# Gate and up products written to PSUM in the order of the weights, with the stride moved into VectorE's transposes

## The chip, the cores and the metric

One core of a Trainium2 chip. The metric is the device time of one execution in microseconds (us), taken as the median of several executions. The kernel is one decode step of a transformer block: 84.2 MB are read from HBM and 1.25 KB are written.

## The reference, cut to what matters

```python
x = A_x                                          # [1, 1, 640], bf16
h = x + attention(layernorm(x), k_cache, v_cache, wq, wo)   # 32 heads of 128, 4096 cached positions
n = layernorm(h)
g = n @ w_gate                                   # 640 -> 1728
u = n @ w_up                                     # 640 -> 1728
h2 = h + (gelu(g) * u) @ w_down                  # 1728 -> 640
```

Everything below is about the last three lines, some 10 us at the end of a kernel of about 205 us.

## The kernel before

1728 = 13 * 128 + 64. In this kernel VectorE and ScalarE take gate and up as columns (128x15 in the timeline below): 128 partitions, with 13 numbers in each (plus two half-used columns for the remaining 64). TensorE makes rows: with the normed vector as the stationary operand (128*1 in the timeline), one matmul gives a row of outputs (416 of them here) along one partition of PSUM. Four such matmuls, at partitions 0, 32, 64 and 96, run side by side: in the trace of before the four start 3 to 4 ns apart, and the next four follow 0.305 us after the first of them. VectorE's transposes (0.68 us for 480 columns) are used here in blocks of 32x32: in the kernel's layout 32 neighbouring columns of a row become 32 partitions.

Partition p of the result is to hold the outputs 13p to 13p+12, since w_down is loaded so that each partition reads 13 whole rows in one piece. A row holds the outputs in the order of the weights: position 13n + c, for n in 0..31. For that layout a block has to take all n of one c side by side. Something has to take a stride of 13, and in this kernel it is the matmul's output:

```python
    def up(ps, w, name):          # 40 matmuls: 5 chunks of the 640 inputs x (four of 416, four of 64 columns)
        landed_once(name)                               # wait for the weights' load
        for j in range(DC):
            for last in range(2):
                for r in range(YR):
                    row = ps[32 * r : 32 * r + 1, :]
                    if last:                            # the remaining 64 outputs, repeated to fill 64 columns
                        ...
                    else:                               # RG = 13 * 32 = 416
                        rhs = w[:, j, r * RG : (r + 1) * RG].rearrange("p (n c) -> p n c", c=FULL)
                        to = row[:, 0:RG].rearrange("q (c n) -> q n c", c=FULL)   # neighbours 32 floats apart
                    inst = PE.matmul(to, lhsT=hc[:, j : j + 1], rhs=rhs, start=False, ...)

    PE.wait_ge(S["dve"], D_HC)
    end("g", up(g_ps, wg_sb, "wg"))
    fill(5)                                             # matmuls that only keep TensorE busy
    end("u", up(u_ps, wu_sb, "wu"))
    fill(4)
    PE.wait_ge(S["dve"], D_HID)
    down = {FULL: "wd0", 0: "wd1", WD[1][0]: "wd2", WD[2][0]: "wd3"}   # WD = ((0, 8), (8, 11), (11, 13))
    for c in range(NFC):                                # 14 groups of four matmuls in all
        if c in down:
            landed_once(down[c])                        # w_down comes in four loads
        ...
```

VectorE's side, with `ps` of 480 columns (416 and 64):

```python
    def turn_rows(col, ps):
        dve(lambda: DVE.transpose(col[:].rearrange("p c n -> p (c n)"), ps), False)
    ...
    wait_pe(T["end", "g"])
    turn_rows(g_col, g_ps)
    ...                     # 1/sd from GpSimd, gelu in nine small operations, with one exp on ScalarE between them
    wait_pe(T["end", "u"])
    turn_rows(u_col, u_ps)
    dve(lambda: DVE.tensor_tensor(hid[:], g_sb[:], u_col[:, :, 0], op=ALU.mult))     # the hidden vector
    wait_pe(T["end", "y"])
    DVE.tensor_tensor(y_row[:], y_ps, h_row[:], op=ALU.add).then_inc(S["y"], 1)      # then the store
```

And the end of the queue of loads, all issued by about 168 us:

```python
    load("wg", wg_sb, ...)
    load("wu", wu_sb, ...)
    SP.wait_ge(S["pe"], ...)                            # the K tile is free
    for i, (a, b) in enumerate(WD):                     # 1280, 480 and 320 KB
        load(f"wd{i + 1}", wd_sb[:, a:b, :], wd_rows[:, a:b, :])
    load("wd0", wd_last, ...)                           # 80 KB
```

The softmax here doesn't subtract the row's maximum and nothing guards it: scores larger than these inputs give would overflow.

Of the kernel before, what the change touches and what calls it, by code (L numbers as in the profile page):

```python
# [9 lines left out]
def kernel(  # L10
# [19 lines left out]
    PE, DVE, ACT, SP, POOL = nc.tensor, nc.vector, nc.scalar, nc.sync, nc.gpsimd  # L30
# [22 lines left out]
    FULL = DF // P  # L53
    LAST = DF - FULL * P
    PER = 2
    NFC = FULL + PER
    HALVES = D // PER
    COLS = NFC * HP
    WD = ((0, 8), (8, 11), (11, 13))
    RG = FULL * HP  # L60
# [102 lines left out]
    def tick(which, inst):  # L163
        inst.then_inc(S[which], 1)
        done[which] += 1
        return done[which]
# [6 lines left out]
    def wait(engine, which, value):  # L173
        if value > 0:
            engine.wait_ge(S[which], value)
# [8 lines left out]
    def landed_once(name):  # L184

        PE.wait_ge(S[name], 16)
        once.append(name)

    def wait_pe(value):
        DVE.wait_ge(S["pe"], value)  # L190

    def dve(make, raw=True):

        if raw:
            wait(DVE, "dve", done["dve"])
        return tick("dve", make())
# [132 lines left out]
    n = EV_RS  # L329
# [15 lines left out]
    n = 0  # L345
# [81 lines left out]
    D_RS = D0 + 4  # L427
    D_SPREAD, D_ROW, D_H, D_HC = D_RS + 4, D_RS + 5, D_RS + 8, D_RS + 10
    D_HV = D_HC + 3
    D_T1 = D_HV + 5  # L430
    D_HID = D_T1 + 7

    def fill(n):

        for _ in range(n):
            PE.matmul(  # L436
                s_bank[0][:], lhsT=ident[:], rhs=e_t[:].rearrange("p j i -> p (j i)"), start=True, stop=True
            )
# [27 lines left out]
    def up(ps, w, name):  # L466


        landed_once(name)
# [4 lines that stand above are left out]
                    if last:  # L474
                        first = FULL * P + r * (HP // PER)
                        rhs = w[:, j, first : first + HP // PER]
                        rhs = rhs.unsqueeze(1).unsqueeze(3).broadcast_to([P, PER, HP // PER, PER])
                        to = row[:, RG:COLS].rearrange("q (b i n) -> q b i n", b=PER, n=PER)
                    else:
                        rhs = w[:, j, r * RG : (r + 1) * RG].rearrange("p (n c) -> p n c", c=FULL)  # L480
                        to = row[:, 0:RG].rearrange("q (c n) -> q n c", c=FULL)
                    inst = PE.matmul(  # L482
                        to,
                        lhsT=hc[:, j : j + 1],
                        rhs=rhs,
                        start=False,
                        stop=(j == DC - 1),
                        skip_group_check=True,
                        tile_position=(0, 32 * r),
                    )  # L490
        return inst

    PE.wait_ge(S["dve"], D_HC)
    end("g", up(g_ps, wg_sb, "wg"))
    fill(5)
# [3 lines that stand above are left out]
    down = {FULL: "wd0", 0: "wd1", WD[1][0]: "wd2", WD[2][0]: "wd3"}  # L499
    order = range(NFC)  # L500
    for c in order:
        if c in down:
            landed_once(down[c])
        for r in range(YR):
            if c < FULL:
                w = wd_sb[:, c, r * YW : (r + 1) * YW]
            elif r // 2 == c - FULL:
                w = wd_last[:, (r % 2) * YW : (r % 2 + 1) * YW]
# [94 lines left out]
    for m in range(NQ):  # L603
        for g in ON_ACT:
            act_copy(m, g)
        for half in range(2):
            ACT.wait_ge(S["pe"], pe_at(m, ("s", half)))
            cols = slice(half * NB // 2, (half + 1) * NB // 2)
            for i in range(QH):
                r, h = slice(i * HP, (i + 1) * HP), QH * m + i  # L610
# [3 lines left out]
            inst.then_inc(S["act_pe"], 1)  # L614
    ACT.wait_ge(S["dve"], D_T1)
    ACT.activation(e2[:], t1[:], AF.Exp, scale=TWO_SQRT_2_OVER_PI).then_inc(S["act"], 1)
# [65 lines left out]
        dve_copies(m + 1, {})  # L682

    def turn_rows(col, ps):
        dve(lambda: DVE.transpose(col[:].rearrange("p c n -> p (c n)"), ps), False)  # L685

    assert done["dve"] == D0
    wait_pe(pe_at(NQ - 1, ("s", 1)))
# [18 lines left out]
    assert var_of(hm, hv) == D_HV  # L707
    wait_pe(T["end", "g"])
    turn_rows(g_col, g_ps)
    DVE.wait_ge(S["r"], 2)  # L710
    dve(lambda: DVE.tensor_scalar(g_sb[:], g_col[:, :, 0], hr[:], None, op0=ALU.mult))
    dve(lambda: DVE.tensor_tensor(t1[:], g_sb[:], g_sb[:], op=ALU.mult))
    dve(lambda: DVE.tensor_scalar(t1[:], t1[:], GELU_C, 1.0, op0=ALU.mult, op1=ALU.add))
    assert dve(lambda: DVE.tensor_tensor(t1[:], t1[:], g_sb[:], op=ALU.mult)) == D_T1
    DVE.wait_ge(S["act"], ACT_ALL)
# [4 lines left out]
    dve(lambda: DVE.scalar_tensor_tensor(g_sb[:], g_sb[:], hr[:], units[:], op0=ALU.mult, op1=ALU.mult))  # L720
    wait_pe(T["end", "u"])
    turn_rows(u_col, u_ps)
    assert dve(lambda: DVE.tensor_tensor(hid[:], g_sb[:], u_col[:, :, 0], op=ALU.mult)) == D_HID
    wait_pe(T["end", "y"])
# [46 lines left out]
```

## Time and profile before

| | before |
|---|---|
| time, median of 3 runs | 205.59 us (205.56 to 205.65) |
| span of the profiled run | 203.8 us |
| gate's 40 matmuls, up's 40 | 2.06 us each |
| one transpose of 480 columns | 0.68 us |
| end of `hc` (input of gate and up) to end of `hid` | 6.26 us |
| last landing of w_down | 200.51 us |
| start of the last group of down-projection matmuls | 200.55 us |

The page of the kernel before: the span, and three of its rows over 40 equal slices of 5.1 us. PEclk is the granted TensorE clock in tenths, DMA the busy share of the DMA engines in tenths, GB/s what they moved.

```profile
span 203.8 us, 7457 instructions
...
PEclk9999999955599559955995599559955995896699
DMA  7999999999999999999999999999999999999991
GB/s 249 394 476 418 390 485 408 412 453 428 434 426 402 436 428 425 444 431 431 431 418 421 448 431 437 431 431 431 431 437 431 405 428 447 444 394 437 428 384 49
```

The DMA engines are at 90% or more in 38 of the 40 slices. The kernel streams from HBM from start to end, so the first question about any change at its tail is when the last load lands.

Two views answer it. First the loads of w_down in the DMA view, with size and the time from issue to landing (the two last ones):

```profile
big<-in_B_w_down_dram SPq DMA_DIRECT2D x1, 320.0 KB, 32.9
big<-in_B_w_down_dram SPq DMA_DIRECT2D x1, 80.0 KB, 32.6
```

Then the queue's timeline: when the last of them was issued (start and duration in us).

```profile
167.89 0.44 SPq L548 DMA_DIRECT2D big<-in_B_w_down_dram  x1
```

167.89 + 32.6 is about 200.5; the trace's own record of landings has 200.51. The piece before it (columns 11 and 12) landed at 200.30.

The timeline of the tail before: start, duration, engine, line, operation, what it writes and reads, shape, count, and in brackets the idle time of the engine before it and what ended it.

```profile
193.00 0.23 DVE L706 TENSOR_SCALAR hc<-h_col,hm 128x5 bf16<-128x5 f32 x1
...
193.29 2.06 PE L482 MATMUL tp_103<-big,hc 128*1 128x416 bf16 x40
...
195.41 0.68 DVE L685 STREAM_TRANSPOSE g_col<-tp_103 128x480 f32<-128x480 f32 x1 [1.60 <-PE tp_103 L482]
196.20 0.23 DVE L711 TENSOR_SCALAR g_sb<-g_col,hr 128x15 f32<-128x15 f32 x1
...
196.47 2.06 PE L482 MATMUL tp_104<-big,hc 128*1 128x416 bf16 x40
...
198.25 0.23 DVE L720 SCALAR_TENSOR_TENSOR g_sb<-g_sb,hr,units 128x15 f32<-128x15 f32 x1
...
198.59 0.68 DVE L685 STREAM_TRANSPOSE u_col<-tp_104 128x480 f32<-128x480 f32 x1
199.31 0.18 DVE L723 TENSOR_TENSOR hid<-g_sb,u_col 128x15 bf16<-128x15 f32 x1
...
199.55 1.24 PE L455 MATMUL tp_105<-big,hid 128*1 128x160 bf16 x56
200.84 0.32 DVE L725 TENSOR_TENSOR y_row<-tp_105,h_row 128x160 bf16<-128x160 f32 x1 [1.35 <-PE tp_105 L455]
```

The starts of the single matmuls in the trace add what this merged view hides. In the down-projection (L455) a group of four follows every 69 ns, from first matmul to first matmul, except for the group of column 11, which comes after 106 ns, at 200.34, and the last one, which comes after 140 ns, at 200.55: each 40 ns behind the landing of its weights. (The prediction below has 96 and 130 ns. These are counted from the last matmul of the group before, where an ordinary gap is 59 ns, so they should not be set beside 69.) So the tail already waits for w_down, by about 0.1 us, though the bracket that would say so is absent. The ends of matmuls are modelled in the profile: it lets the matmul before the last group end at 200.65, after the landing at 200.51, so TensorE does not count as idle there. For the same reason the page's chain of work that ended last does not name the load either:

```profile
PE 18%; ACT 4%; DVE 1%; issue 0%
ACT ex L611 4%; PE tp_103 L255 3%; PE tp_104 L255 2%; PE tp_106 L255 2%; PE tp_105 L255 2%; PE o L281 2%; PE sa L436 2%; PE sa L268 2%; PE tp_103 L482 1%; PE tp_104 L482 1%; PE a L292 1%; PE tp_105 L455 1%; DVE u_col L685 0%; PE tp_106 L304
```

### The profile page before, as it was taken

Reading aid. Unit: us, or ns where it says so; the run is one execution under the profiler, and the core shown is the slowest. Engines: PE = TensorE matmul, PEld = TensorE weight load, DVE = VectorE, ACT = ScalarE, POOL = GpSimd, SP = SyncE. Lnnn points to the kernel's source line nnn. Section 1 sums busy time; section 2 is a strip of 40 time slices with the busy share of each in tenths; the row PEclk is TensorE's granted clock in tenths of the full one; section 3 lists DMA queues with packets and bytes.
Section 4 is the critical chain, followed back from the end, with each engine's and each line's share of the span. In section 5 each row is a group of like instructions: output and inputs, shape, how many; then the busy total and the mean of one; then the engine's idle time right before and its main releaser. Section 6 shows DMA issues by size and latency. Waiting matters only on the chain. (4 is left out here: it accounts for less than half of the span.)

```text
span 203.8 us, 7457 instructions
## 1 busy us (share of the span) xinstructions
PE 152.3 (75%) x3453; PEld 139.1 (68%) x3453; DVE 70.6 (35%) x163; ACT 81.6 (40%) x179; POOL 20.3 (10%) x20
## 2 busy tenths in 40 slices
PE   0003689854996399869985998389849989998994
PEld 0001179754996399869975998389849989997332
DVE  4003127300480049104800670038105801742452
ACT  0000326531386118623770477018712862674000
POOL 8301000620000000800000008000000000000010
PEclk9999999955599559955995599559955995896699
DMA  7999999999999999999999999999999999999991
GB/s 249 394 476 418 390 485 408 412 453 428 434 426 402 436 428 425 444 431 431 431 418 421 448 431 437 431 431 431 431 437 431 405 428 447 444 394 437 428 384 49
DMA packets 4058, 84.38 MB, mean 414 GB/s; under 512 B 464, under 2 KB 592, under 8 KB 848
## 3 DMA queue, kind: packets, MB, share of 16 engines
q1 hardware_dynamic: 4048, 84.23, 96.8%
q8 instruction: 8, 0.13, 0.3%
q14 instruction: 2, 0.02, 0.0%
HBM read 84.23 MB, written 0.00 MB: 413 GB/s over the span
## 5 line engine op out<-in xcount | busy, mean ns | idle before, releaser
L281 PE MATMUL o<-ex,big 128*128 128x4 bf16 x1024 | 29.7, 166 | 11.5 <-ACT ex L611 6.5
L281 PEld LDWEIGHTS o<-ex,big 128*128 128x128 bf16 x1024 | 28.3, 102 | 12.9 <-ACT ex L611 7.7
L597 ACT COPY big<-tp_104 128x1024 bf16<-128x1024 bf16 x16 | 16.2, 1012 | 48.3 <-PE tp_104 L255 48.3
L255 PE MATMUL tp_103<-ident,big 128*128 128x128 bf16 x256 | 24.9, 255 | 10.9 <-PEq L180 10.9
L255 PEld LDWEIGHTS tp_103<-ident,big 128*128 128x128 bf16 x256 | 20.4, 118 | 11.4 <-issue 11.4
L255 PE MATMUL tp_104<-ident,big 128*128 128x128 bf16 x256 | 24.1, 249 | 0.0
L255 PE MATMUL tp_105<-ident,big 128*128 128x128 bf16 x256 | 23.3, 244 | 0.0
L255 PE MATMUL tp_106<-ident,big 128*128 128x128 bf16 x256 | 23.1, 242 | 0.0
L624 DVE COPY big<-tp_103 128x1024 bf16<-128x1024 bf16 x24 | 16.5, 688 | 18.5 <-PE tp_103 L255 18.5
L542 POOL COPY wo<-wo_in 128x5120 bf16<-128x5120 bf16 x3 | 13.3, 4450 | 94.2 <-PE a L292 94.2
L255 PEld LDWEIGHTS tp_104<-ident,big 128*128 128x128 bf16 x256 | 19.9, 115 | 0.0
L255 PEld LDWEIGHTS tp_105<-ident,big 128*128 128x128 bf16 x256 | 19.2, 112 | 0.0
L255 PEld LDWEIGHTS tp_106<-ident,big 128*128 128x128 bf16 x256 | 18.9, 111 | 0.0
L268 PE MATMUL sb<-q_78,big 128*128 128x4 bf16 x512 | 14.3, 164 | 5.0 <-issue 5.0
L624 DVE COPY big<-tp_106 128x1024 bf16<-128x1024 bf16 x24 | 16.6, 691 | 3.4 <-PE tp_106 L255 2.9
L597 ACT COPY big<-tp_105 128x1024 bf16<-128x1024 bf16 x16 | 16.2, 1014 | 3.0 <-PE tp_105 L255 2.9
L268 PEld LDWEIGHTS sb<-q_78,big 128*128 128x128 bf16 x512 | 13.6, 96 | 5.1 <-issue 5.1
L611 ACT ACTIVATE ex<-sa 32x64 bf16<-32x64 f32 x32 | 9.8, 306 | 11.4 <-PE sa L268 11.2
L268 PE MATMUL sa<-q_78,big 128*128 128x4 bf16 x512 | 14.0, 164 | 0.0
L624 DVE COPY big<-tp_105 128x1024 bf16<-128x1024 bf16 x16 | 11.1, 691 | 8.4 <-PE tp_105 L255 8.1
L268 PEld LDWEIGHTS sa<-q_78,big 128*128 128x128 bf16 x512 | 13.5, 96 | 0.6
L681 DVE COPY o_raw<-o 128x4 f32<-128x4 f32 x4 | 0.7, 163 | 36.9 <-PE o L281 36.9
(111 smaller groups left out, 117.3 us busy)
## 6 DMA issues: line engine op xcount, KB each, us to landing
big<-in_A_v_cache_dram SPq DMA_DIRECT2D x8, 4096.0 KB, 33.1
big<-in_A_k_cache_dram SPq DMA_DIRECT2D x7, 4096.0 KB, 26.1
big<-in_A_wq_dram SPq DMA_DIRECT2D x1, 5120.0 KB, 15.5
wo_in<-in_A_wo_dram SPq DMA_DIRECT2D x4, 1280.0 KB, 27.1
big<-in_A_k_cache_dram SPq DMA_DIRECT2D x2, 2048.0 KB, 23.9
big<-in_B_w_gate_dram SPq DMA_DIRECT2D x1, 2160.0 KB, 39.0
big<-in_B_w_up_dram SPq DMA_DIRECT2D x1, 2160.0 KB, 43.6
big<-in_B_w_down_dram SPq DMA_DIRECT2D x1, 1280.0 KB, 31.8
```

The source lines that it names most:

```text
L255: inst = PE.transpose(tp_b[g % NBANK][:, b * DH : (b + 1) * DH], kt[slot][:, g * GRP + b, :], ident[:])
L268: inst = PE.matmul(s_ps[half][:, j % (NB // 2), :], lhsT=kt[slot][:, j, :], rhs=q8[:, slot * QH : (slot + 1) * QH], start=True, stop=True,)
L281: inst = PE.matmul(o_ps, lhsT=vt[slot][:, j, :], rhs=e_t[:, j, :], start=(j == 0), stop=(j == NB - 1))
L542: POOL.tensor_copy(wo_t[:], wo_in[:]).then_inc(S["wo"], 1)
L597: ACT.copy(group(m % SLOTS, g), tp_g[g % NBANK]).then_inc(S["act_pe"], 1)
L611: inst = ACT.activation(e_t[r, cols, i], s_ps[half][r, :, i], AF.Exp, scale=SCALE, accum_out=rs_all[r, half, h : h + 1])
L624: DVE.tensor_copy(group(m % SLOTS, g), tp_g[g % NBANK]).then_inc(S["dve_pe"], 1)
L681: event(DVE.tensor_copy(o_raw[:, HG * turn : HG * turn + QH], o_ps))
```

## The change

Its intent: TensorE writes its 416 columns at unit step, and VectorE, whose transpose of `h_col` already reads at a step of 20 bytes (0.47 us), takes the step of 13 floats (52 bytes). The 64 remaining columns were in another order already, so each transpose becomes two.

```diff
-    D_T1 = D_HV + 5
-    D_HID = D_T1 + 7
+    D_T1 = D_HV + 6
+    D_HID = D_T1 + 8
@@ in up()
-                        rhs = w[:, j, r * RG : (r + 1) * RG].rearrange("p (n c) -> p n c", c=FULL)
-                        to = row[:, 0:RG].rearrange("q (c n) -> q n c", c=FULL)
+                        rhs = w[:, j, r * RG : (r + 1) * RG]
+                        to = row[:, 0:RG]
@@ in turn_rows()
-        dve(lambda: DVE.transpose(col[:].rearrange("p c n -> p (c n)"), ps), False)
+        dve(lambda: DVE.transpose(col[:, 0:FULL], ps[:, 0:RG].rearrange("q (p c) -> q c p", c=FULL)), False)
+        dve(lambda: DVE.transpose(col[:, FULL:NFC].rearrange("p c n -> p (c n)"), ps[:, RG:COLS]), False)
```

Nothing else moves; the number of matmuls stays, and VectorE has two instructions more.

## The prediction

> **What bounds the kernel now.** The slices show the DMA engines at 90% or more up to the last slices (84.2 MB in a span of 203.8 us). The chain of waits names short PE, ScalarE and VectorE pieces at the end, but what counts is a load: in the DMA view the last piece of w_down is issued at 167.9 us and lands 32.6 us later, at about 200.51. The down-projection's matmuls agree: groups of four follow each other every 69 ns from 199.55, but the one that needs the third w_down piece comes after 96 ns (landing 200.30) and the last after 130 ns, at 200.55, 40 ns after the last landing. So it already waits about 0.1 us for weights. An earlier hidden vector gains nothing; one later by up to 0.1 us costs nothing.
>
> **PE: removed.** In the timeline a step of gate (four 416-column matmuls, four 64-column ones) takes 0.378 us: 0.305 from the 416s to the 64s, 0.07 for those, at a granted clock of 1.00. 0.305/416 is 0.73 ns a column; the 160-column matmuls with unit-stride output take 0.069/160 = 0.43. [...] With unit stride the 416s should take about 0.18: 0.13 us less a step, 0.65 for each of gate and up. Gate's saving moves the first transpose from 195.41 to about 194.76 (POOL's rstd ends before, at 194.44). Up's saving is worth nothing: up then ends near 197.2, long before VectorE asks.
>
> **VectorE: added.** One transpose of 480 unit-stride columns takes 0.683 us, so about 0.18 fixed. The strided transpose that exists (h_col, 160 columns, 20-byte step, SBUF) takes 0.469, where unit rate would give 0.35: 0.71 cycles more per element, as between the two reductions of the same 128 elements, 0.27 and 0.37. I assume the same for the 52-byte step in PSUM: 416 columns take 0.93 us (0.62 if the stride is free there, 1.1 if it costs double). The 64-column transpose takes 0.25, of which 0.08 may overlap. Together 1.10 us (0.8 to 1.3), against 0.68.
>
> **Critical path.** The gate chain from the transpose's end to the gated product, 2.39 us, stays. Up's transpose now runs right behind it. Down-projection starts at 194.76 + 1.10 + 2.39 + 0.04 + 1.10 + 0.28 = about 199.67, against 199.55. The exchange nearly cancels: +0.84 on VectorE, -0.65 on gate's matmuls, -0.1 of slack at up. The last group of four would start at 200.57, against 200.55 set by the loads. At 0.8 for the pair the time is unchanged, at 1.3 it is +0.4.
>
> **Predicted time:** 205.7 us, 205.4 to 206.2. Faster by over 2%: 0.005; within 2%: 0.985; slower by over 2%: 0.01.
>
> **What would show it.** Right: gate's and up's matmul groups fall from 2.06 to about 1.4 us; the strided transpose is 0.93 us; no VectorE idle before up's transpose; down-projection starts within 0.3 us of 199.55; last landing still 200.5. Wrong on the loads: an earlier down-projection ends earlier. Wrong on VectorE: a strided transpose of 0.62 (time unchanged, longer waits for w_down) or over 1.1.
>
> **What would make it wrong.** PE now idles about 1.6 us before down-projection; if the clock falls, its groups take 121 to 133 ns, as in the attention projection at 0.50, and the end moves by 0.8.

0.18 us is 416 times the 0.43 ns a column read off the 160-column groups. That the stride is what makes the 416s slow was inference from 0.73 against 0.43 ns; the run of after bears it out. The 0.18 us fixed and the unit rate of VectorE's transposes were estimates too, shown only later: in after_probes 64, 160 and 416 columns at unit step in SBUF took 245, 346 and 611 ns, which makes 1.04 ns per element and 0.18 us fixed. A cycle in its VectorE paragraph stands for that 1.04 ns.

## The result, and the profile after

| | before | after |
|---|---|---|
| time, median of 6 runs each | 205.62 us (205.48 to 206.26) | 205.55 us (205.43 to 205.69) |
| ratio, 95% interval | | 0.999 (0.9976 to 1.0004) |
| gate's matmuls, up's matmuls | 2.06, 2.06 us | 1.20, 1.20 us |
| transposes of gate, from the first start to the last end | 0.68 us | 0.75 us |
| end of `hc` to end of `hid` | 6.26 us | 5.33 us |
| last landing of w_down | 200.51 us | 200.38 us |
| last group of down-projection starts | 200.55 us | 200.42 us |

A ratio here is the mean time of one kernel's fast runs over that of the other's in the same rounds, so it is not quite the ratio of the medians quoted.

The time is the same. The chain of small steps that the change touches is 0.93 us shorter, and none of it arrives. The page after:

```profile
span 203.7 us, 7459 instructions
...
PEclk9999969955695569856985698569855995995797
DMA  7999999999999999999999999999999999999991
GB/s 249 418 452 418 394 482 409 415 454 451 415 410 412 455 409 431 438 438 438 418 418 427 442 431 438 438 438 418 425 444 431 409 425 447 438 400 437 427 386 50
```

The stream of loads looks as it did. The timeline of the tail after:

```profile
192.41 0.23 DVE L708 TENSOR_SCALAR hc<-h_col,hm 128x5 bf16<-128x5 f32 x1
...
192.69 1.20 PE L482 MATMUL tp_103<-big,hc 128*1 128x416 bf16 x40
...
193.94 0.62 DVE L686 STREAM_TRANSPOSE g_col<-tp_103 128x416 f32<-128x416 f32 x1 [0.73 <-PE tp_103 L482]
194.48 0.21 DVE L687 STREAM_TRANSPOSE g_col<-tp_103 128x64 f32<-128x64 f32 x1
194.80 0.23 DVE L713 TENSOR_SCALAR g_sb<-g_col,hr 128x15 f32<-128x15 f32 x1
...
195.16 1.20 PE L482 MATMUL tp_104<-big,hc 128*1 128x416 bf16 x40
...
196.85 0.23 DVE L722 SCALAR_TENSOR_TENSOR g_sb<-g_sb,hr,units 128x15 f32<-128x15 f32 x1
197.00 0.61 DVE L686 STREAM_TRANSPOSE u_col<-tp_104 128x416 f32<-128x416 f32 x1
197.53 0.21 DVE L687 STREAM_TRANSPOSE u_col<-tp_104 128x64 f32<-128x64 f32 x1
197.78 0.19 DVE L725 TENSOR_TENSOR hid<-g_sb,u_col 128x15 bf16<-128x15 f32 x1
...
198.35 0.72 PE L455 MATMUL tp_105<-big,hid 128*1 128x160 bf16 x32 [1.02 <-DMA big<-in_B_w_down_dram]
...
199.42 0.38 PE L455 MATMUL tp_105<-big,hid 128*1 128x160 bf16 x12 [0.35 <-DMA big<-in_B_w_down_dram]
...
200.22 0.45 PE L455 MATMUL tp_105<-big,hid 128*1 128x160 bf16 x12 [0.42 <-DMA big<-in_B_w_down_dram]
200.72 0.32 DVE L727 TENSOR_TENSOR y_row<-tp_105,h_row 128x160 bf16<-128x160 f32 x1 [2.75 <-PE tp_105 L455]
```

`hid` is done at 197.97, 1.5 us earlier than before, and the down-projection then stops three times for a load of w_down: it starts at 198.35, not at 198.03, because the first piece landed at 198.21; it waits again for the second piece, and again for the third. Its last group follows the last landing by 40 ns, exactly as before. Of the 1.5 us, 0.93 are the change's; 0.60 are not: `hc` ended at 192.64 in this execution against 193.24, for a reason that comes up below.

The landing is found the same way, the loads first (the two last):

```profile
big<-in_B_w_down_dram SPq DMA_DIRECT2D x1, 320.0 KB, 33.2
big<-in_B_w_down_dram SPq DMA_DIRECT2D x1, 80.0 KB, 32.9
```

and the issue of the last:

```profile
167.44 0.43 SPq L548 DMA_DIRECT2D big<-in_B_w_down_dram  x1
```

167.44 + 32.9 is about 200.4 (200.38 in the record of landings). The page's chain that ended last now starts its shares with a load instead of a list of engines. The second fence is the end of the same chain in order of time (start, duration, what):

```profile
DMA 16%; PE 7%; SPq 0%; DVE 0%; issue 0%
```

```profile
166.97 33.20 DMA big<-in_B_w_down_dram
200.17 0.04 issue
200.22 0.48 PE tp_105 L455 x12
```

The load that it names is the third piece, landed at 200.17, ahead of the last three groups. The wait for the last piece, 140 ns from group to group in place of 69, stays hidden as it did before; the landing at 200.38 and the start at 200.42 show it.

### The profile page after: what moved, and what is told of

It reads as the page before. It is cut to its first block, busy times and chain, and to the rows that moved or that the text cites. A ratio compares the mean times of both kernels' runs of the same rounds, so it can differ in the third digit from the quotient of the medians.

```text
span 203.7 us, 7459 instructions
## 1 busy us (share of the span) xinstructions
PE 149.8 (74%) x3453; PEld 137.5 (68%) x3453; DVE 70.8 (35%) x165; ACT 81.5 (40%) x179; POOL 20.3 (10%) x20
## 5 line engine op out<-in xcount | busy, mean ns | idle before, releaser
L255 PE MATMUL tp_103<-ident,big 128*128 128x128 bf16 x256 | 24.4, 252 | 13.0 <-PEq L180 13.0
L255 PEld LDWEIGHTS tp_103<-ident,big 128*128 128x128 bf16 x256 | 20.0, 117 | 13.5 <-issue 13.4
L255 PE MATMUL tp_104<-ident,big 128*128 128x128 bf16 x256 | 23.8, 247 | 0.0
L255 PE MATMUL tp_105<-ident,big 128*128 128x128 bf16 x256 | 23.2, 243 | 0.0
L255 PE MATMUL tp_106<-ident,big 128*128 128x128 bf16 x256 | 22.8, 241 | 0.0
L255 PEld LDWEIGHTS tp_104<-ident,big 128*128 128x128 bf16 x256 | 19.5, 113 | 0.0
L255 PEld LDWEIGHTS tp_105<-ident,big 128*128 128x128 bf16 x256 | 19.0, 111 | 0.0
L255 PEld LDWEIGHTS tp_106<-ident,big 128*128 128x128 bf16 x256 | 18.8, 110 | 0.0
```

Of the source, the lines that this page charges most:

```text
L255: inst = PE.transpose(tp_b[g % NBANK][:, b * DH : (b + 1) * DH], kt[slot][:, g * GRP + b, :], ident[:])
```

## The experiments

Theory A: the end is set by the last landing of w_down. The change does shorten the chain from `hc` to `hid`, by about 0.93 us, but that chain has slack. The rivals are written into the expectations: B, that VectorE ate the gain; C, that the tail does not count at all; D, that the spread of times comes from the loads.

### 1 and 2. Take the bound away: most of w_down is not read

Both kernels, with w_down read for 16 of 128 partitions. The result is wrong on purpose (relative error 0.045); the waits and the work stay.

```diff
-        load(f"wd{i + 1}", wd_sb[:, a:b, :], wd_rows[:, a:b, :])
+        load(f"wd{i + 1}", wd_sb[0:16, a:b, :], wd_rows[0:16, a:b, :])
-    load("wd0", wd_last, B_w_down[FULL * P : DF, :].rearrange("i (b d) -> (i b) d", b=PER))
+    load("wd0", wd_last[0:16, :], B_w_down[FULL * P : FULL * P + 8, :].rearrange("i (b d) -> (i b) d", b=PER))
```

> The kernel before, but w_down is read for 16 of its 128 partitions only (wrong result on purpose), so its loads end near 196 us and the down-projection waits for nothing but the hidden vector. Theory A (the last landing of w_down sets the end; the change shortens the gate chain by about 0.93 us but off the critical path): the end was late by only about 0.1 us here, so 205.4 to 205.6 us, ratio to before 0.998 to 1.0. Rival B (the change's gain on PE was eaten by VectorE, the chain is as long as before): the same here; the next run tells them apart.

> The changed kernel with the same cut of w_down's loads (wrong result on purpose). Theory A: the shortened chain now reaches the end: about 0.9 us under the run before_short_wd, so 204.4 to 204.7 us, ratio to before 0.994 to 0.996; from the end of hc to the end of hid 5.3 us against 6.3. Rival B: within 0.2 us of before_short_wd, ratio 0.998 to 1.0.

Measured: the kernel before with short loads took 205.85 us (205.18 to 206.36, ratio to before 1.001, 0.9992 to 1.0029); the changed one 204.90 us (204.48 to 205.56, ratio 0.9971, 0.9952 to 0.9991). Five rounds on the same chip as runs 3 and 4. The difference of the medians is 0.95 us, where B expected at most 0.2. The absolute times are 0.2 to 0.3 us above the ranges expected, and both spread over more than 1 us. From the timelines, the down-projection of before and of after, now in one piece with no wait for a load:

```profile
199.63 1.14 PE L455 MATMUL tp<-big,hid 128*1 128x160 bf16 x56
```

```profile
198.56 1.14 PE L455 MATMUL tp<-big,hid 128*1 128x160 bf16 x56
```

In the changed kernel `hc` to `hid` took 5.60 us here rather than 5.33, because w_up landed 1.1 us later than in the full kernel (196.24 against 195.11) and up waited for it. Why cutting w_down makes w_up land later was not looked into. So the cut put another load's landing in the way of the changed kernel, and the 0.95 us is no clean measure of the chain: the two traced spans differ by 1.08 us, 0.65 from the shorter chain and 0.42 from an `hc` that ended earlier in that execution. Why the kernel before with short loads was rather slower than with full ones (205.85 against 205.51 us, not clear of noise), when it was to be no slower, was not looked into either.

So the change makes the chain faster, and where the chain sets the end, the kernel is faster. B falls.

### 3, 4 and 5. Use the slack up: delay the hidden vector

Up's transpose is done twice, or four times, all loads in place and the result right. The semaphore counts (`D_HID`) are raised to match.

```diff
-    turn_rows(u_col, u_ps)
+    for _ in range(2):        # 4 in after_late3
+        wait(DVE, "dve", done["dve"])
+        turn_rows(u_col, u_ps)
```

> The kernel before with up's transpose done twice, which makes the hidden vector 0.73 us later (0.68 and a wait); result right. Theory A: only about 0.1 us of slack, so 0.6 us slower: 206.2 us, ratio 1.003. Rival C (the end has slack for other reasons, the tail of the kernel doesn't count): ratio 1.000.

> The changed kernel with up's two transposes done twice, about 0.8 us later; result right. Theory A: the hidden vector, 2.3 us before the last landing less 0.9 of matmuls, has 1.2 us or more of slack, so no change against the changed kernel: 205.5 us, ratio to before 0.999 to 1.0, and last group of the down-projection still at the last landing. Rival B: no slack was made, so 0.6 us slower, ratio 1.003.

> The changed kernel with up's two transposes done four times, 2.35 us later; result right. Theory A: more than the slack, so the hidden vector sets the end again: hid ends at about 200.3, last group of the down-projection at about 201.4 us in the profile against 200.4, 206.5 us, ratio 1.005, and a spread of some tenths of a us. The idle time before w_down landings is gone. Rival C (the tail does not count): ratio 1.000.

Measured: before, twice: 206.10 us (205.54 to 206.47), ratio 1.0021 (1.0002 to 1.0039). After, twice: 205.92 us (205.64 to 206.29), ratio 1.0019 (1.0002 to 1.0036). After, four times, in a later set: 207.45 us (206.52 to 208.00), ratio 1.0075 (1.0051 to 1.0099).

The first and the third are slower as A says, which leaves nothing of C, but the third by 1.9 us where 1.0 was expected; what follows the table below bears on that. The second missed: A expected no change, and the times alone look like B. The profiled execution of it (205.82 us) does not. Its timeline:

```profile
198.99 0.18 DVE L727 TENSOR_TENSOR hid<-g_sb,u_col 128x15 bf16<-128x15 f32 x1
...
199.23 0.93 PE L455 MATMUL tp<-big,hid 128*1 128x160 bf16 x44 [1.80 <-DVE hid L727]
...
200.37 0.44 PE L455 MATMUL tp<-big,hid 128*1 128x160 bf16 x12 [0.21 <-DMA big<-in_B_w_down_dram]
```

The delayed `hid` is done at 199.18, and the down-projection still stops for a load before its last three groups. That execution was bound by the landing. The two slowest executions, at 206.28 and 206.29, left no trace.

### What all the traces say together

Each profiled execution has an end of the span, a last landing and an end of `hid`. All in us from the start of the span:

| execution | end of `hc` | end of `hid` | last landing | span | span - landing | span - `hid` |
|---|---|---|---|---|---|---|
| before | 193.24 | 199.49 | 200.51 | 203.78 | **3.28** | 4.29 |
| after | 192.64 | 197.97 | 200.38 | 203.66 | **3.27** | 5.69 |
| before_short_wd | 193.32 | 199.57 | 197.96 | 203.76 | 5.80 | **4.19** |
| after_short_wd | 192.90 | 198.50 | 197.84 | 202.68 | 4.84 | **4.18** |
| before_late1 | 192.97 | 199.95 | 200.40 | 204.13 | 3.73 | **4.18** |
| after_late1 | 192.87 | 199.18 | 200.53 | 203.81 | **3.28** | 4.63 |
| after_late3 | 194.06 | 201.92 | 200.62 | 206.12 | 5.50 | **4.19** |
| after_again | 191.96 | 197.79 | 200.34 | 203.61 | **3.27** | 5.82 |
| after_small_first | 194.30 | 199.63 | 200.81 | 204.23 | 3.41 | 4.60 |
| gate_only | 194.02 | 199.41 | 200.53 | 203.80 | **3.27** | 4.39 |
| gate_only_short_wd | 192.49 | 199.67 | 198.00 | 203.86 | 5.86 | **4.19** |
| up_only_short_wd | 192.31 | 198.93 | 197.63 | 203.12 | 5.49 | **4.19** |
| after_probes | 192.62 | 197.95 | 200.42 | 203.69 | **3.28** | 5.75 |
| after_write_patterns | 193.61 | 199.06 | 200.59 | 203.86 | **3.28** | 4.80 |

The end is always the later of two: the last landing plus 3.28 us (the last group, the addition, the store) or the end of `hid` plus 4.19 us (all 14 groups, then the same). The one exception, after_small_first, has a larger piece of w_down last and so two groups behind the landing in place of one: 3.41. No execution is off by more than 0.02 us. `hid` has slack as long as it is done 4.19 - 3.28 = 0.91 us before the last landing. Before had 0.1 us of it in the profiled run; after had 1.5.

The second thing in the table is the column of `hc`, which no edit here touches: it moves by 2.3 us from one execution to the next. The granted clock moves too. The trace records its steps: half clock ran from 184.95 to 191.78 us in the run of before, 184.1 to 191.0 in after, 186.3 to 193.1 in after_small_first, and `hc` follows the step up by 1.2 to 1.7 us in these, and in 11 of the 14 executions. In the other three (after_again, gate_only_short_wd, up_only_short_wd) half clock began earlier, at 182.6 to 183.2, lasted 10.24 us, and `hc` ended 0.8 to 0.9 us before the step up. No run changed the clock's phase alone, so that it moves `hc` is argued from these traces and not shown by an experiment. The lengths between steps are 6.83, 10.24 and 13.65 us, multiples of 3.41, and where the steps fall differs from run to run; what sets them was not shown. With `hc` as late as the 194.30 seen, after_late1 would end `hid` at 194.30 + 6.31 = 200.61 and the span at 204.80, 1.0 us over its profiled run; this estimate from the traces covers its slow executions, but they themselves were not traced. The same sum covers after_late3: its six spans, 204.6 to 206.1 us, less 4.19 and the 7.87 us from `hc` to `hid` in its trace, ask for an `hc` between 192.5 and 194.1, all within what was seen. Its traced execution, the slowest of the six, had an `hc` 1.4 us later than the run of after, and four transposes cost 0.2 us more than expected.

### 6. The changed kernel again

> The changed kernel unaltered, for more runs of it beside the kernel before. Theory A, sharpened by the runs so far: the start of the gate chain moves by some tenths of a us from run to run (where the granted clock's steps fall); the kernel before, with 0.1 us of slack, shows that in its times (4 of 17 runs so far at or above 205.8 us), the changed kernel, with 1.2 us or more, does not: median 205.4 to 205.6, ratio 0.999 to 1.0, no run above 205.8 us. Rival D (the spread comes from the loads themselves): as many late runs as the kernel before, some at 205.8 to 206.3 us.

Measured: 205.59 us (205.40 to 205.88), the kernel before beside it 205.59 us (205.46 to 206.14), ratio 0.9999 (0.9987 to 1.0012). The median is as expected; one run of five was above 205.8, where none was expected. Over the three sets with rounds, 6 of 28 runs of the kernel before and 1 of 11 of the changed kernel were at or above 205.8 us. That points the way that slack would, but it is too few to call shown; the late run itself left no trace.

### 7. Try to turn the slack into time: another order of w_down's loads

```diff
+    load("wd0", wd_last, B_w_down[FULL * P : DF, :].rearrange("i (b d) -> (i b) d", b=PER))
     for i, (a, b) in enumerate(WD):
         load(f"wd{i + 1}", wd_sb[:, a:b, :], wd_rows[:, a:b, :])
-    load("wd0", wd_last, B_w_down[FULL * P : DF, :].rearrange("i (b d) -> (i b) d", b=PER))
```

> The changed kernel with the smallest load of w_down (80 KB, packets of 640 bytes) issued ahead of the others in place of last; result right. Theory A: the end follows the last landing. The order does not change the bytes, so the last landing should move by 0.2 us at most (200.2 to 200.4), and the time with it: 205.3 to 205.5 us, ratio 0.998 to 0.9995. If the tail's fall of the DMA share comes from the small packets, it is the better end of that.

Measured: 205.76 us (205.71 to 206.01), ratio 1.0004 (0.9991 to 1.0017). It was to be 0.1 us faster and is, if anything, 0.2 slower: the last landing in the trace is at 200.81, not 200.4, and two groups follow it. That trace is of the slowest of the five runs; the spans of the others, 203.9 to 204.0 us, less 3.41 put their last landing at about 200.5 to 200.6 (an estimate). The new order brought no gain; that it is worse is not clear of the noise. No version that beats both kernels came out.

### 8, 9 and 10. One half of the change at a time

Gate as changed and up as before, without and with the cut of w_down, and the reverse with the cut. The edit puts the two forms of `up()` and of `turn_rows()` behind a condition:

```diff
+                        if name == "wg":        # "wu" in up_only_short_wd
                             rhs = w[:, j, r * RG : (r + 1) * RG]
                             to = row[:, 0:RG]
+                        else:
+                            rhs = w[:, j, r * RG : (r + 1) * RG].rearrange("p (n c) -> p n c", c=FULL)
+                            to = row[:, 0:RG].rearrange("q (c n) -> q n c", c=FULL)
```

> The kernel of after_short_wd with up as it was before (strided writes, one transpose), gate as changed; right but for the cut of w_down. Theory A: gate's matmuls give nearly all: from the end of hc to the end of hid about 5.3 to 5.6 us (gate 0.86 us less, 0.07 more for its second transpose); up's 2.06 us of matmuls may then end after the gate chain is done, and cost up to 0.3. Rival: the gain comes from up as much as from gate: about 5.8 us.

> The kernel of before_short_wd with up as changed, gate as before (right but for the cut of w_down). Theory A, in which gate's matmuls are on the chain and up's are hidden behind it: from the end of hc to the end of hid about 6.2 us, against 6.26 before and 5.3 changed; VectorE does not wait for up. Rival (the gain comes from up): about 5.4 us.

> Gate as changed, up as before, all loads as they were; result right. Theory A: the end stays at the last landing plus 3.28 us in the profile, whatever the chain does; hid comes before the last landing less 0.91. Up's matmuls then end about 2.06 us after w_up's landing or gate's last filler, at about 197.2 us, when VectorE, done with gate, has waited 0.1 to 0.3 us: from the end of hc to the end of hid 5.4 to 5.7 us. The record's claim that up's saving is worth nothing holds if there is no wait at all.

With the cut, gate alone: `hc` to `hid` 7.18 us, a miss. w_up landed at 196.61 there, up's slow 2.06 us began only then, and VectorE stood idle 1.29 us for it; gate's own matmuls also ran partly at half clock (1.46 us in place of 1.20). So this run does not weigh the halves. With all loads in place, gate alone: 5.39 us, span at the landing plus 3.27. That is the test that counts, and it says that gate's half gives all of it but 0.06 us. The profile shows no long wait for up there, but not none: up's transpose starts 0.035 us after the gated product ends, at 198.50, just behind the end of up's matmuls, where in the changed kernel it starts 0.084 us before that end. So up's faster matmuls are worth about 0.12 us of the chain, and its second transpose takes back 0.06. With the cut, up alone: 6.62 us, of which 0.5 is a longer wait for gate's matmuls, which began at half clock (2.29 us in place of 2.06; VectorE idle 2.10 us before gate's transpose against 1.60); that would leave 6.1 against the 6.2 expected.

gate_only also shows the worth of the slack: with its `hc` at 194.02, the kernel before's 6.26 us would have put `hid` at 200.28 and the end at 204.47, by the table's rule; the span was 203.80.

### 11. What a stride costs VectorE

Ten transposes added to VectorE's idle start, from PSUM and SBUF, at unit step and with strides; result right.

```diff
+    dve(lambda: DVE.transpose(turned_to[:, 0:416], in_psum[:, 0:416]))
+    dve(lambda: DVE.transpose(turned_to[:, 0:416].rearrange("p (c n) -> p c n", n=HP), in_psum[:, 0:416].rearrange("q (p c) -> q c p", c=13)))
+    ...        # the same two from SBUF, four of 160 columns at a step of 1 and 5, two of 64 at 2 and 1
```

> The changed kernel with ten transposes added on VectorE at its idle start (result right): 416 columns at unit step and at 52 bytes, 160 at unit step and at 20 bytes, each from PSUM and from SBUF, and 64 from SBUF at 8 bytes and at unit step. Theory P (a stride costs in SBUF but not in PSUM): PSUM 0.61 us at both steps of 416 and 0.34 at both of 160; SBUF 0.61 and 0.34 at unit step, 0.92 at 52 bytes, 0.47 at 20 bytes. Rival Q (the step of 52 bytes is free, that of 20 is not, or the 0.47 of the h transpose is no stride's cost): SBUF 0.61 at 52 bytes too, or 0.47 at unit step too.

Its timeline, VectorE only (`sa` is in PSUM, `u_col` in SBUF; odd rows unit step, even rows strided; the two of 64 columns are left out):

```profile
4.23 0.62 DVE L219 STREAM_TRANSPOSE g_col<-sa 128x416 f32<-128x416 f32 x1
4.88 0.62 DVE L220 STREAM_TRANSPOSE g_col<-sa 128x416 f32<-128x416 f32 x1
5.53 0.61 DVE L221 STREAM_TRANSPOSE g_col<-u_col 128x416 f32<-128x416 f32 x1
6.17 0.89 DVE L222 STREAM_TRANSPOSE g_col<-u_col 128x416 f32<-128x416 f32 x1
7.10 0.35 DVE L223 STREAM_TRANSPOSE g_col<-sa 128x160 f32<-128x160 f32 x1
7.49 0.35 DVE L224 STREAM_TRANSPOSE g_col<-sa 128x160 f32<-128x160 f32 x1
7.87 0.35 DVE L225 STREAM_TRANSPOSE g_col<-u_col 128x160 f32<-128x160 f32 x1
8.25 0.46 DVE L226 STREAM_TRANSPOSE g_col<-u_col 128x160 f32<-128x160 f32 x1
```

416 columns from PSUM take 0.62 us at unit step and at 52 bytes (617 and 616 ns). From SBUF they take 611 and 894 ns: 0.68 ns more per element. 160 columns: 350 and 350 ns from PSUM, 346 and 462 ns from SBUF. Theory P holds for these fp32 transposes, one execution each: the cost shows in SBUF and not in PSUM. At 8 bytes SBUF's step cost nothing either (246 and 245 ns for 64 columns).

### 12. What a stride costs TensorE's write

Gate written in pairs of neighbours, each pair 128 bytes from the one before; up at a step of 8 bytes. Wrong order on purpose. (The expectation says 104 bytes. By the edit, where `n` counts 16, the step from pair to pair is 16 * 2 floats, 128 bytes: the distance of the single columns in the kernel before.)

```diff
+                        if name == "wg":
+                            rhs = rhs.rearrange("p (n c b) -> p n c b", c=FULL, b=2)
+                            to = row[:, 0:RG].rearrange("q (c n b) -> q n c b", c=FULL, b=2)
+                        else:
+                            rhs = rhs.rearrange("p (b n) -> p b n", b=2)
+                            to = row[:, 0:RG].rearrange("q (n b) -> q b n", b=2)
```

> The changed kernel with gate's 416 columns written to PSUM in pairs of neighbours, the pairs 104 bytes apart, and up's at a step of two columns, 8 bytes (wrong result on purpose). [...] pairs run as fast as unit step, a step of gate every 0.205 us, group 1.2 us; the 8-byte step costs two cycles a column as the 128-byte step did, a step of up every 0.375 us, group 2.06 us. If any step other than one costs: both 2.06 us. If only large steps cost: up 1.2 us.

(The cut took out the condition of the first case; what it tests is whether only a step that breaks the pairs costs. A cycle there is the time of a column at unit step, 0.43 ns by the 160-column groups of the down-projection.)

Its timeline, TensorE only, gate then up:

```profile
193.66 1.20 PE L487 MATMUL tp<-big,hc 128*1 128x416 bf16 x40
...
195.97 2.06 PE L487 MATMUL tp<-big,hc 128*1 128x416 bf16 x40
```

Pairs run as fast as unit step, 1.20 us; a step of 8 bytes, which breaks the pairs, costs as much as 128 bytes did, 2.06. A step of gate came every 0.205 us, of up every 0.378. (`hc` to `hid` took 5.45 us here, with up slow and each transpose in two parts: 0.12 more than in the changed kernel, the worth of up's matmuls again.) The comparison with the reference passed all the same, though gate and up were permuted differently: its tolerance is too coarse to see an error of order in this part, and "result right" in these texts is to be read with that. That the changed kernel puts each number where the one before did follows from the two access patterns, not from that comparison.

## Why the prediction was right or wrong

**The time was right** (205.7 predicted, 205.4 to 206.2; 205.55 measured), and so was the reason that decides it: "An earlier hidden vector gains nothing". The reading that found it was a small one, two gaps of 106 and 140 ns in a row of 69, each 40 ns behind a landing. Experiments 1 and 2 removed the bound and a gain appeared; the table of 14 executions gives the rule.

**The sum under it was wrong in two terms, in the same direction.** The prediction had the exchange nearly cancel and the down-projection start 0.12 us later; the runs show the chain 0.93 us shorter. That the time came out right is owed to the bound, not to the sum.

- *"I assume the same for the 52-byte step in PSUM: 416 columns take 0.93 us."* It took 0.617 us, and the pair of transposes 0.75 us rather than 1.10. The 0.71 cycles per element (0.74 ns: 0.469 against 0.35 us over 160 elements) were read off transposes and reductions in SBUF; for SBUF they nearly hold (0.894 us measured for 416), but reads of PSUM showed no such cost at 20 and 52 bytes (350 against 350 ns for 160 columns, 616 against 617 ns for 416). The prediction named 0.62 "if the stride is free there" and took the other.
- *"0.13 us less a step, 0.65 for each of gate and up."* A step went from 0.378 to 0.205 us, and a group from 2.06 to 1.20: 0.86. The prediction split a step at the start of the 64-column matmuls (0.305 and 0.07 us) and took the second part for theirs. But after the change those matmuls take 0.028 us, so 0.04 of the 0.07 went with the strided write too. Over the whole step, the strided write cost (0.378 - 0.205)/416 = 0.42 ns a column on top of the 0.205/480 = 0.43 ns that a column takes at unit step (the 160-column groups of the down-projection, 160 columns in 69 ns, give the same 0.43). So it took about twice as long a column, not 1.7 times, as 0.73 against 0.43 had it. As an estimate from these figures, a step was worth 416 * 2 + 64 = 896 columns at unit step, 0.38 us.
- *"No VectorE idle before up's transpose"*, *"last landing still 200.5"* (200.38), the clock: right. Up's transpose ran right behind gate's chain, and the last landings lay between 200.34 and 200.62 wherever w_down's loads were unchanged. The feared fall of the clock before the down-projection did not come: its groups still took 69 ns.
- *"Down-projection starts within 0.3 us of 199.55"*: wrong, 198.35, and it was ready 0.3 us before that.
- *"Up's saving is worth nothing"*: nearly. Up's faster matmuls are worth about 0.12 us of the chain (gate_only, after_write_patterns), 0.06 after its second transpose; none of it reaches the end.

The ledger of the chain, from the two timelines: `hc` to gate's first transpose -0.87 us, gate's transposes +0.07, gelu 0.00, the gap before up's transpose -0.19 (before, VectorE waited there for up's matmuls), up's transposes to `hid` +0.07. The sum, -0.92, is the 6.26 to 5.33 us within rounding.

Open: why some executions of after_late1 were slow, beyond the estimate above; whether the changed kernel has fewer late executions than the one before; why w_up lands later when w_down is cut.

## What to carry to other kernels

Before costing a change at the tail of a kernel that streams from HBM, look for the last landing and for the small irregular gaps behind it: the end here was the later of two chains (the last landing plus 3.28 us, `hid` plus 4.19), and shortening one of them is worth at most the time by which it is the later one. Here a shortening of 0.93 us bought slack and no time, so the next gain is to be looked for in the loads. And cost a stride in the memory where it falls: reads of SBUF, reads of PSUM and writes to PSUM each gave another answer for the same permutation (at 52 bytes 0.68 ns more per element from SBUF and none from PSUM; written at 128 bytes, 0.42 ns more per column).
